# The first sixteen attention items with the exponential taken out of PSUM and the value product turned; a second weight piece in every second preamble round

## The chip, the cores and the metric

The kernel runs on one core of one Trainium2 chip. The metric is the device time of one execution in microseconds (us), median of three runs. The engines are TensorE (PE in the profile; its weight loads are listed apart as PEld), VectorE (DVE), ScalarE (ACT), GpSimd (POOL) and SyncE (SP), which here only issues DMAs. Each engine works off its own instructions in a fixed order.

## What is computed

A causal attention with a window of 128 keys and a linear distance bias, and behind it two two-layer MLPs with the same 2304 tokens, all in float32:

```python
# attention: q, k, v of shape (4, 8, 576, 64)
scores = scale * np.matmul(q, k.transpose(0, 1, 3, 2))
scores = np.where(mask, scores + bias[None], -1000000000.0)
scores = scores - np.max(scores, axis=-1, keepdims=True)
attn = np.exp(scores)
attn = attn / (np.sum(attn, axis=-1, keepdims=True) + 1e-09)
out = np.matmul(attn, v)          # then heads side by side: 2304 tokens x 512
# first MLP, 512 -> 2048 -> 512
h = x @ w_in
g = np.maximum(h, 0.0) + alpha * np.minimum(h, 0.0)
x = g @ w_out
# second MLP, 512 -> 2048 -> 512
h = x @ w_in
g = h * (1.0 / (1.0 + np.exp(-1.702 * h)))
out = g @ w_out
```

## The kernel before

The attention is cut into 64 **items**, one for a batch, a query range (unit 0: 256 queries, unit 1: 320 queries) and a head. Items 0 to 15 (`n < FP`), the heads of the first two batches, are the **float32 items**: their matmuls run on float32 operands. Later items split each operand into a rounded high and a low part and multiply with both. A pair of items (two neighbouring heads) fills one of four 128-row slices of the input `x` of the first MLP, again as high part `xh` and low part `xl`.

One float32 item goes through these steps before the change. `a_qk` (L342) makes the scores of two chunks of 128 queries, 128 and 256 keys wide, in PSUM. `a_bias` (L362) adds the bias on VectorE, writes `tt` in SBUF and leaves the row minimum of the negated scores in `st`. `a_exp` (L378) takes the exponential on ScalarE with the minimum as bias and gathers the row sums. `a_recip` (L386, L387) and `a_norm` (L398) divide on VectorE. `a_trans` (L411) turns three 128x128 blocks on TensorE into PSUM, `a_pt_hi` (L418) copies them to `pt`, and `a_av` (L432) multiplies: the values, laid into one half of a 128-wide tile `vz` whose other half is zero, are the stationary operand, and the product of two heads accumulates to 128 rows by 256 queries, the layout that the MLP wants. `a_x3` (L479, L107) casts it to `xh` and `xl`.

The MLP weights come in as 64-bit numbers and are decoded on the chip. The first MLP has 32 **pieces**, two for each of its 16 slices `f` of the hidden dimension (one of `w_in`, one of `w_out`). A piece costs two ScalarE passes (`w_scale`, L147 and L150), a shift (L154) and an add (L159) on VectorE, and the split into a high part `wh` (a cast, L102 on ScalarE, for two pieces L103 on VectorE) and a low part `wl` (L107 on VectorE).

The program begins with a **preamble** of ten rounds (L741). A round issues the steps of several items, each at another stage, and one weight piece; rounds 0, 4 and 8 issue a second piece. Then the first MLP runs over nine blocks of 256 tokens, each in 16 steps. Step `(k, f)` issues the hidden matmuls of slice `f` (`m1_h`, L493, tile `h`), the activation (L508, L518), its split (`gh`, L522, and `gl`, L107) and, two slices later, the output matmuls (`m1_o`, L544). In block `k = 0` the rest of the 32 pieces is decoded, and half an attention item goes with each step. A scheduler takes the written program and moves instructions of each engine ahead of one another; only the weight steps keep their written order among themselves. So the order on the engines isn't the order in the text.

## Time and profile before

| | us |
|---|---|
| median of 3 runs | 948.61 |
| the three runs | 948.21, 948.61, 950.05 |
| profiled execution, time | 951.22 |
| profiled execution, span | 949.4 |
| TensorE busy | 926.7 (98% of the span) |
| VectorE busy | 687.6 (72%) |
| ScalarE busy | 526.7 (55%) |

The profile is one execution. Its own time of 951.22 lies 2.61 above the median, and 1.8 us of it lie outside the span. Busy shares are means over very different stages: the second MLP fills the last 400 us and has little for VectorE and ScalarE to do, while in the first 105 us VectorE and ScalarE are nearly full. Stretches in time, and the chain of waits, tell more than the means.

### The profile page before, as it was taken

Reading aid. Unit: us, or ns where it says so; the run is one execution under the profiler, and the core shown is the slowest. Engines: PE = TensorE matmul, PEld = TensorE weight load, DVE = VectorE, ACT = ScalarE, POOL = GpSimd, SP = SyncE. Lnnn points to the kernel's source line nnn. Section 1 sums busy time; section 2 is a strip of 40 time slices with the busy share of each in tenths; the row PEclk is TensorE's granted clock in tenths of the full one; section 3 lists DMA queues with packets and bytes.
Section 4 is the critical chain, followed back from the end, with each engine's and each line's share of the span. In section 5 each row is a group of like instructions: output and inputs, shape, how many; then the busy total and the mean of one; then the engine's idle time right before and its main releaser. Section 6 shows DMA issues by size and latency. Waiting matters only on the chain.

```text
span 949.4 us, 17872 instructions
## 1 busy us (share of the span) xinstructions
PE 926.7 (98%) x6536; PEld 862.2 (91%) x6536; DVE 687.6 (72%) x1743; ACT 526.7 (55%) x1325; POOL 89.7 (9%) x127
## 2 busy tenths in 40 slices
PE   6899999999999999999999999999999999999997
PEld 3698899999999999999988888888898899999997
DVE  6898876778888888888457753685333798878876
ACT  5999866667667676676344443564232553433333
POOL 1100211122222222222000000000000000000000
PEclk9999999999999999999999999999999999999999
DMA  9666511223222222221023344665332333433323
GB/s 242 205 217 209 183 54 55 66 68 91 69 67 91 67 68 91 67 90 44 1 89 110 112 128 169 203 227 199 117 124 99 134 134 117 151 133 132 132 72 112
DMA packets 44041, 112.45 MB, mean 118 GB/s; under 512 B 5041, under 2 KB 15153, under 8 KB 43953
## 3 DMA queue, kind: packets, MB, share of 16 engines
q1 hardware_dynamic: 43952, 111.31, 36.1%
q8 instruction: 51, 0.84, 0.4%
q14 instruction: 38, 0.30, 0.1%
HBM read 82.98 MB, written 28.31 MB: 117 GB/s over the span
## 4 chain that ended last, share of the span: by engine, by line
PE 91%; DVE 2%; issue 1%; ACT 0%; DVEq 0%; ACTq 0%
PE h L493 21%; PE h L591 21%; PE p L658 18%; PE o L544 17%; PE p L544 5%; PE x L444 3%; PE pt L411 3%; PE s L351 1%; PE s L352 1%; PE s L342 1%; DVE wl L107 0%; DVE wd L159 0%; ACT oh L102 0%; PE x L432 0%; DVE wd L154 0%
## 5 line engine op out<-in xcount | busy, mean ns | idle before, releaser
L493 PE MATMUL h<-xh,wh 128*128 128x256 f32 (+1 forms) x512 | 151.9, 298 | 1.4 <-ACT xh L479 1.4
L493 PE MATMUL h<-xh,wl 128*128 128x256 f32 (+1 forms) x512 | 152.3, 298 | 0.0
L493 PE MATMUL h<-xl,wh 128*128 128x256 f32 (+1 forms) x512 | 151.4, 296 | 0.0
L658 PE MATMUL p<-wh,oh 128*128 128x256 f32 x504 | 136.3, 284 | 1.0 <-ACT oh L102 0.6
L658 PE MATMUL p<-wl,oh 128*128 128x256 f32 x504 | 136.2, 283 | 0.0
L544 PE MATMUL o<-gh,wl 128*128 128x256 f32 x448 | 127.5, 286 | 0.0
L544 PE MATMUL o<-gh,wh 128*128 128x256 f32 x448 | 125.9, 286 | 0.7 <-ACT gh L522 0.7
L544 PE MATMUL o<-gl,wh 128*128 128x256 f32 x448 | 125.5, 281 | 1.1 <-DVE gl L107 1.1
L658 PE MATMUL p<-wh,ol 128*128 128x256 f32 x504 | 119.2, 283 | 0.4 <-DVE ol L107 0.4
L591 PE MATMUL h<-x2h,wh 128*128 128x512 f32 (+1 forms) x320 | 117.9, 368 | 0.0
L591 PE MATMUL h<-x2l,wh 128*128 128x512 f32 (+1 forms) x320 | 117.8, 368 | 0.0
L591 PE MATMUL h<-x2h,wl 128*128 128x512 f32 (+1 forms) x320 | 117.7, 368 | 0.0
L605 DVE TENSOR_TENSOR g<-h,sg 128x512 f32<-128x512 f32 (+1 forms) x80 | 51.0, 638 | 90.7 <-ACT sg L601 90.5
L601 ACT ACTIVATE sg<-h 128x512 f32<-128x512 f32 (+1 forms) x80 | 44.4, 555 | 108.5 <-PE h L591 108.3
L493 PEld LDWEIGHTS h<-xh,wh 128*128 128x128 f32 x512 | 96.3, 189 | 5.2 <-ACT xh L479 1.9
L493 PEld LDWEIGHTS h<-xh,wl 128*128 128x128 f32 x512 | 96.6, 189 | 3.9 <-DVE wl L107 0.6
L493 PEld LDWEIGHTS h<-xl,wh 128*128 128x128 f32 x512 | 97.0, 189 | 3.0 <-issue 0.3
L658 PEld LDWEIGHTS p<-wh,oh 128*128 128x128 f32 x504 | 96.5, 192 | 2.1 <-ACT oh L102 2.0
L658 PEld LDWEIGHTS p<-wl,oh 128*128 128x128 f32 x504 | 96.7, 192 | 0.1
L518 DVE SCALAR_TENSOR_TENSOR g<-n,beta,h 128x256 f32<-128x256 f32 x112 | 53.2, 475 | 54.1 <-ACT n L508 53.8
L508 ACT ACTIVATE n<-h 128x256 f32<-128x256 f32 x112 | 42.8, 383 | 87.8 <-PE h L493 87.3
L658 PEld LDWEIGHTS p<-wh,ol 128*128 128x128 f32 x504 | 86.5, 192 | 0.7 <-DVE ol L107 0.6
(105 smaller groups left out, 2203.0 us busy)
## 6 DMA issues: line engine op xcount, KB each, us to landing
ws<-in_w_in_dram SPq DMA_DIRECT2D x32, 512.0 KB, 3.9
ws<-in_w_out_dram SPq DMA_DIRECT2D x32, 512.0 KB, 3.7
raw<-in_u_dram SPq DMA_DIRECT2D x32, 512.0 KB, 3.5
g2d<-g SPq DMA_DIRECT2D x32, 512.0 KB, 3.1
gr<-g2d SPq DMA_DIRECT2D x32, 512.0 KB, 3.2
raw<-in_u_dram SPq DMA_DIRECT2D x16, 320.0 KB, 2.8
wd<-x2d SPq DMA_DIRECT2D x36, 128.0 KB, 2.9
out_dram<-ob SPq DMA_DIRECT2D x16, 256.0 KB, 3.4
```

The source lines that it names most:

```text
L342: nc.tensor.matmul(o[:, :keys], raw[:, c0 : c0 + rows], raw[:, 256 + kk : 256 + kk + keys], start=True, stop=True)
L351: nc.tensor.matmul(o[:, :n_], q, kh[:, ks : ks + n_], start=True, stop=False)
L411: nc.tensor.transpose(banks[bank][:, dst : dst + P], src, ident)
L444: nc.tensor.matmul(x[:, oc : oc + nq], v, p[:, col : col + nq], start=(i == 0 and k == 0), stop=(i == len(js) - 1 and k == 1), skip_group_ ...
L493: nc.tensor.matmul(ph, w[:, 0, c * P : (c + 1) * P], x[:, c, r : r + n], start=(c == 0 and i == 0), stop=(c == NC - 1 and i == 2),)
L508: nc.scalar.activation(n, ph, AF.Relu, scale=-1.0)
L518: nc.vector.scalar_tensor_tensor(g, n, beta[:, f : f + 1], ph, op0=ALU.mult, op1=ALU.add)
L544: nc.tensor.matmul(o, w[:, 1, c * P : (c + 1) * P], g, start=(f == 0 and (k == KM or c % 2 == 0) and i == 0), stop=(f == NF - 1 and i == 2 ...
L591: nc.tensor.matmul(ph[:, :n], w[:, f % 2, c * P : (c + 1) * P], x[:, c, :n], start=(c == 0 and i == 0), stop=(c == NC - 1 and i == 2),)
L601: nc.scalar.activation(sg[:, :n], ph[:, :n], AF.Sigmoid, scale=1.702)
L605: nc.vector.tensor_tensor(g[:, f % 2, :n], ph[:, :n], sg[:, :n], op=ALU.mult)
L658: nc.tensor.matmul(o[:, m, :], g[:, a, m * P : (m + 1) * P], w, start=(p == 0 and m == 0 and i == 0), stop=(p == NF // 2 - 1 and i == 2), ...
```

## The change

For the float32 items, the order of the steps is turned around. `f_sub` subtracts from the row minimum (one chunk on VectorE, L383, one on ScalarE, L381) in place of the exponential. The three blocks are transposed unnormalised, and `f_exp` (L389) takes the exponential of the transposed scores straight out of PSUM on its way to `pt`, so that it takes the place of the copy. `f_av` (L463) makes the blocks of `pt` the stationary operand and streams the values, 64 columns and one column of ones, so that the row sums come out as column 65. `f_div` (L474 to L476) divides once for a pair of heads, straight out of PSUM into `xq`, and two more transposes (L520) bring the result into the layout of `x`. The recip and norm steps, and the row-sum reads behind the exponential, fall away for these items. An item is one round shorter: what belonged to item `n - 2` now belongs to `n - 1`. And the preamble's second piece comes in rounds 0, 2, 4, 6 and 8.

```diff
@@ f_sub, f_exp
+            if i:
+                nc.scalar.activation(t, t, AF.Identity, bias=s[:rows, i : i + 1], scale=-1.0)
+            else:
+                nc.vector.tensor_scalar(t, t, s[:rows, i : i + 1], -1.0, op0=ALU.subtract, op1=ALU.mult)
...
+            x, c, w = st["t", n][0]
+            nc.scalar.activation(pts[n % 2], x[:, :w], AF.Exp)
@@ f_av, f_div in place of a_av for these items
+        if h % 2 == 0:
+            st["xq", n // 2] = early("o0", n, "xq").rearrange("p c (h t) -> p c h t", h=2)
+        x = st["xq", n // 2]
+        pt, vz = pts[n % 2], vzs[n % 2]
+        for c, j, col in ((0, 0, 0), (1, 0, 128), (1, 1, 256)):
+            nc.tensor.matmul(
+                x[:, c, h % 2, : D + 1], pt[:, col : col + P], vz[:, j, :],
+                start=(c == j == h % 2 == 0), stop=(c == j), skip_group_check=True,
+            )
...
+        nc.vector.tensor_scalar(r, x[:, :, :, D], 1e-9, None, op0=ALU.add)
+        nc.vector.reciprocal(f, r)
+        nc.vector.tensor_tensor(xq, x[:, :, :, :D], f.unsqueeze(3).to_broadcast([P, 2, 2, D]), op=ALU.mult)
-            for j in range(2):
-                nc.tensor.matmul(
-                    x[:, j * P : 256], vz[:, j, :], pt[:, j * 256 : 256 + j * P],
...
@@ a_x3
-            xp = st["x", n]
+            xp = early("o1", n, "x").rearrange("p c t -> p (c t)")
+            for i in range(2):
+                nc.tensor.transpose(xp[:, i * P : (i + 1) * P], xq[:, i, :, :], ident)
@@ the preamble's rounds
-        a_av(n - 2)
+        f_exp(n - 1)
         a_split_v(n)
...
         a_bias(n)
+        f_sub(n)
         w("split")
-        a_exp(n)
-        a_recip(n - 1)
+        f_av(n - 1)
         w("shift")
-        a_norm(n - 1, "dve")
-        a_trans(n - 1)
         w("add")
         w_ahead()
+        f_div(n - 1)
+        a_trans(n, True)
         w("scale")
-        a_x3(n - 2)
-        if n % 4 == 0:
+        if n % 2 == 0:
             w("split")
             w("shift")
-        a_pt_hi(n - 1, 0)
-        a_pt_hi(n - 1, 1)
+        a_x3(n - 1)
```

`early` takes a PSUM bank that the first MLP's output sums use only later (for items 0 to 7) or one of the four attention banks. In block `k = 0` the float32 items 10 to 15 go the same new way.

The scheduler's order moves with it. On VectorE, the first MLP's first block can start once the fourth `xl` is written, the slice of heads 6 and 7. In these rows `wl` with a number is the low half of the weights of one slice `f`, `st` the row statistics, `g` and `gl` the activation and its low half. Before, VectorE at the fourth `xl`, with ten `wl` already written:

```order
L159 ISA wd<-ws,wd 128x1024 x2
L386 TENSOR_SCALAR st_149<-st_149 128x2
L387 RECIPROCAL st_149<-st_149 128x2
L398 TENSOR_SCALAR tt_147<-tt_147,st_149 128x128
L398 TENSOR_SCALAR tt_147<-tt_147,st_149 128x256
L107 TENSOR_TENSOR xl<-x,xh 128x256
L107 TENSOR_TENSOR wl_498<-wd,wh_497 128x512
```

Now, VectorE at the fourth `xl`, with nine `wl` already written:

```order
L474 TENSOR_SCALAR st_149<-xq 128x4
L159 ISA wd<-ws,wd 128x1024
L475 RECIPROCAL st_149<-st_149 128x4
L476 TENSOR_TENSOR xq<-xq,st_149 128x256
L107 TENSOR_TENSOR wl_432<-wd,wh_431 128x512
L154 TENSOR_SCALAR wd<-wd 128x512
L362 ISA tt_146,st_148<-s,relht 128x128
L362 ISA st_148 128x1
L362 ISA tt_146,st_148<-s,relht 128x256
L362 ISA st_148 128x1
L107 TENSOR_TENSOR xl<-x,xh 128x256
```

The normalising pair L398 is gone there, and the division of a pair (L474 to L476) stands in its place. The other place is VectorE at the last pieces of the first MLP's weights, those of slice 15, whose first `wl` (of `w_in`) the hidden matmuls of step `(0, 15)` need. Before, `wl_1123` being slice 14 and `wl_1229` slice 15:

```order
L107 TENSOR_TENSOR wl_1123<-wd,wh_1122 128x512
L362 ISA tt_147,st_149<-s,relt 128x128
L362 ISA st_149 128x1
L362 ISA tt_147,st_149<-s,relt 128x256
L362 ISA st_149 128x1
L107 TENSOR_TENSOR wl_1123<-wd,wh_1122 128x512
L107 TENSOR_TENSOR wl_1229<-wd,wh_1228 128x512
L107 TENSOR_TENSOR gl<-g,gh 128x256
L107 TENSOR_TENSOR ptl<-pt,pth 128x384
```

Now, with `wl_1080` slice 14 and `wl_1140` slice 15; `xp` and `ptl`, `q` are steps of the split items behind the float32 ones:

```order
L107 TENSOR_TENSOR wl_1080<-wd,wh_1079 128x512
L154 TENSOR_SCALAR wd<-wd 128x512
L565 SCALAR_TENSOR_TENSOR g<-n,beta,h 128x256
L362 ISA tt_147,st_149<-s,relt 128x128
L362 ISA st_149 128x1
L362 ISA tt_147,st_149<-s,relt 128x256
L362 ISA st_149 128x1
L510 TENSOR_TENSOR xp<-x,tb 64x256
L159 ISA wd<-ws,wd 128x1024
L107 TENSOR_TENSOR wl_1140<-wd,wh_1139 128x512
L318 SCALAR_TENSOR_TENSOR q<-raw_144,q 64x256
L107 TENSOR_TENSOR ptl<-pt,pth 128x384
```

The `wl` of slice 15 moved behind steps of four more split items: by then 22 items have passed the bias step, before it was 18. On TensorE the same has happened: ahead of the first matmul that reads the low half of slice 15 there now stand 12 hidden and 12 output matmuls more of the MLP, 12 more transposes, and the score and value matmuls of four split items. Before, TensorE at that matmul (`wl_1229`):

```order
L544 MATMUL o_696<-gh,wh_1059 128x256
L544 MATMUL o_697<-gh,wh_1059 128x256
L444 MATMUL x<-pth,vp_1318 128x256
L493 MATMUL h<-xh,wl_1229 128x256
L493 MATMUL h<-xh,wh_1228 128x256
```

Now (`wl_1140`), with the hidden matmuls of the next block (`wl_232`) ahead of it:

```order
L540 MATMUL h<-xh,wl_232 128x256
L489 MATMUL x<-pth,vp_1321 128x256
L591 MATMUL o_717<-gh,wh_1079 128x256
L591 MATMUL o_718<-gh,wh_1079 128x256
L540 MATMUL h<-xh,wl_1140 128x256
L540 MATMUL h<-xh,wh_1139 128x256
```

The row moved from 6008 matmuls before the end to 5940. Further down, the last 5696 TensorE rows stand in the same order in both kernels.

## Rows read from the trace of the kernel before

**Rows 1.** Stretches: us; busy us of PE, PEld, DVE, ACT, POOL; clock, DMA.

```profile
10.00:47.00 37.00, 30.70 (x115) 21.70 (x116) 31.19 (x107) 31.10 (x82) 4.54 (x10) 1.00 0.81 225
47.00:90.00 43.00, 42.99 (x320) 38.85 (x321) 38.84 (x112) 38.60 (x96) 2.94 (x7) 1.00 0.66 211
90.00:105.10 15.10, 12.54 (x88) 10.79 (x86) 14.94 (x45) 14.99 (x40) 2.28 (x5) 1.00 0.74 233
105.10:946.00 840.90, 837.19 (x6009) 788.99 (x6008) 599.97 (x1471) 438.53 (x1102) 77.56 (x92) 1.00 0.32 106
```

**Rows 2.** Waits of PE from 105.2 to the end: us, times, longest.

```profile
PE p L658 <- ACT oh L102: 0.6, 1, 0.6
PE p L658 <- DVE ol L107: 0.4, 1, 0.4
```

**Rows 3.** Timeline: start, us, engine, line, op; the fourth `xl`, last pieces, matmul behind.

```profile
46.85 0.42 DVE L107 TENSOR_TENSOR xl<-x,xh 128x256 fp32r<-128x256 f32 x1
...
103.78 1.28 DVE L107 TENSOR_TENSOR wl<-wd,wh 128x512 fp32r<-128x512 f32 x2
...
105.12 0.39 PE L493 MATMUL h<-xh,wl 128*128 128x256 f32 x1
```

**Rows 4.** Chain that ended last, 85 to 112 us: start, us to the next step.

```profile
85.49 0.65 PE x L432 x4
...
90.04 0.34 DVE tt L362
90.39 0.60 DVE wl L107
90.99 0.34 DVE wd L154
91.33 0.39 DVE g L518
91.72 0.60 DVE wd L159
92.32 0.08 DVE st L386
...
93.54 0.46 DVE tt L398 x2
...
95.93 0.20 DVE tt L362
...
97.12 0.36 DVE q L317
...
99.54 0.34 DVE gl L107
...
100.61 0.41 issue
...
101.52 0.14 issue
...
108.07 1.45 PE h L493 x12
...
111.40 0.09 PE s L351
...
111.61 0.22 PE pt L411 x2
```

**Rows 5.** ACT groups, 9 to 105.1: shape, count, busy us, mean ns, idle before.

```profile
L378 ACT ACTIVATE tt<-tt,st 128x256 f32<-128x256 f32 x17 | 8.5, 503 | 0.0
L378 ACT ACTIVATE tt<-tt,st 128x128 f32<-128x128 f32 x17 | 6.8, 403 | 0.0
L378 ACT ACTIVATION_READ_ACCUMULATOR tt<-tt,st 128x1 f32 x33 | 6.4, 194 | 0.0
```

**Rows 6.** One PE shape, first from 3 to 32, then from 33 to 100 us.

```profile
L342 PE MATMUL s<-raw 64*128 64x256 f32 x8 | 4.2, 631 | 0.0
...
L342 PE MATMUL s<-raw 64*128 64x256 f32 x16 | 5.0, 390 | 0.0
```

More of the change, by code (lines that the diff above doesn't have):

```diff
@@ L373, in a_exp, with f_sub, f_exp @@
     @stage
+    def f_sub(n, b, u, h, U):
+        if n >= FP:
+            return
+        tt, s = tts[n % 2], sts[n % 2]
+        for i, (c0, rows, kk, keys) in enumerate(U["chunks"]):
+            t = tt[:rows, i * 256 : i * 256 + keys]
+            if i:
+                nc.scalar.activation(t, t, AF.Identity, bias=s[:rows, i : i + 1], scale=-1.0)
+            else:
+                nc.vector.tensor_scalar(t, t, s[:rows, i : i + 1], -1.0, op0=ALU.subtract, op1=ALU.mult)
+    @stage
+    def f_exp(n, b, u, h, U):
+        if n < FP:
+            x, c, w = st["t", n][0]
+            nc.scalar.activation(pts[n % 2], x[:, :w], AF.Exp)
+    @stage
     def a_exp(n, b, u, h, U):
         tt, s = tts[n % 2], sts[n % 2]
+        if n < FP:
+            return
         for i, (c0, rows, kk, keys) in enumerate(U["chunks"]):
@@ L391, in a_norm @@
         tt, s = tts[n % 2], sts[n % 2]
-        for i, (c0, rows, kk, keys) in enumerate(U["chunks"]):
+        for i, (c0, rows, kk, keys) in enumerate(U["chunks"] if n >= FP else ()):
             t = tt[:rows, i * 256 : i * 256 + keys]
@@ L415, in a_pt_hi @@
     def a_pt_hi(n, b, u, h, U, i):
-        if i <= u:
+        if i <= u and n >= FP:
             x, c, w = st["t", n][i]
-            nc.scalar.copy(pts[n % 2] if n < FP else ar["pth"][:, c : c + w], x[:, :w])
+            nc.scalar.copy(ar["pth"][:, c : c + w], x[:, :w])
     @stage
@@ L424, in a_pt_lo, with early, f_av, f_div @@
             sub("dve", ar["ptl"][:, c : c + w], x[:, :w], ar["pth"][:, c : c + w])
+    def early(tag, n, name):
+        pool, tag = (pso, tag) if n < H else (ps_a, "a")
+        return pool.tile([P, 2, T1], F32, tag=tag, name=name)
+    @stage
+    def f_av(n, b, u, h, U):
+        if n >= FP:
+            return
+        if h % 2 == 0:
[7 more added lines that the diff above has]
+            )
+    @stage
+    def f_div(n, b, u, h, U):
+        if n >= FP or h % 2 == 0:
+            return
+        s, x = sts[n % 2], st["xq", n // 2]
+        r, f = (s[:, i : i + 4].rearrange("p (c h) -> p c h", c=2) for i in (8, 12))
+        nc.vector.tensor_scalar(r, x[:, :, :, D], 1e-9, None, op0=ALU.add)
+        nc.vector.reciprocal(f, r)
+        nc.vector.tensor_tensor(xq, x[:, :, :, :D], f.unsqueeze(3).to_broadcast([P, 2, 2, D]), op=ALU.mult)
     @stage
@@ L707, in tile_window_attention__then__two_mlps @@
     for t in vzs:
-        nc.gpsimd.memset(t, 0.0)
+        nc.gpsimd.memset(t, 1.0)
     for t in sts:
@@ L778, in tile_window_attention__then__two_mlps @@
     a_split(n)
-    for i in range(2):
-        a_pt_lo(n - 2, i)
-    a_recip(n - 1)
-    a_norm(n - 1, "dve")
-    a_av(n - 2)
-    a_x1(n - 2)
-    a_x2(n - 2)
-    a_x3(n - 2)
+    f_exp(n - 1)
     at0.close()
```

28 lines of the change are left out of this document (18 added, 10 removed).

## The prediction

> **What bounds the kernel now.** I read the busy times by stretch first [rows 1]. From 105.1 us on TensorE is busy without a break: 6009 matmuls, 837.2 of 840.9 us, and in all that time it waits 1.0 us for other engines [rows 2]. Nothing that VectorE or ScalarE saves there shortens anything. Ahead of that point TensorE has gaps: 6.3 us of 37 between 10 and 47, none between 47 and 90, 2.6 of 15.1 between 90 and 105.1 [rows 1]. In this last stretch VectorE and ScalarE are full (14.94 and 14.99 of 15.1), and the chain of waits runs over VectorE, with weight steps, bias, split, and two short pauses in it [rows 4]. The last gap ends at one instruction. VectorE writes two `wl` from 103.78 to 105.06, the second is the low half of `w_in` for slice 15, and at 105.12 TensorE starts the hidden matmul that reads it [rows 3]. From there the order of all TensorE work is a full queue. So the time is the moment at which this `wl` is there, plus the TensorE work that stands behind the matmul that reads it. I predict these two numbers and nothing else.
>
> **What of the change costs nothing.** GpSimd's memset and value copies (POOL is busy 4.54 of 37 us early on [rows 1]) and the DMA issues on SP, which carry the same transfers in nearly the same order, are covered; uncovered, a late value copy would hold only the value product of one item. Past the point where the orders agree again the kernels are the same, TensorE is full there, and VectorE's lighter queue is worth zero.
>
> **VectorE's queue up to the fourth `xl`.** With it the first block of the MLP can start; it begins at 46.85 before [rows 3]. I count what the order puts ahead of it, and price each kind by its distance to the next start in the chain [rows 4]: `wl` 0.60, add 0.60, shift 0.34, a 256-wide operation on two tensors 0.34, bias 0.34 and 0.20 for its two chunks, the 256-wide half of the normalising pair 0.46 - 0.20 = 0.26, a row-statistics step 0.08, of which I make 0.10 for the dependent ones. Away: 10 normalising halves (2.6), 12 statistics steps net (1.2), 3 adds, 2 shifts and 1 `wl` (3.1, only put off). New: 4 divisions (1.4; the trace has none, and `gl`, of the same shape out of PSUM or SBUF, is the nearest row; 0.3 to 0.5 each) and one more bias (0.5). Sum: -5.0 us, so with the same pauses the block starts at 41.8. The 128-wide subtraction costs what the 128-wide half of the normalising pair cost.
>
> **VectorE's queue up to the deciding `wl`.** The same count there: away 12 normalising halves (3.1) and 8 statistics steps (0.8). New: 8 divisions (2.7), one add, shift and `xl` (1.3), one `g` and `gl` (0.7), and the steps of four more split items: 4 biases (2.2), 4 normalising 128-wide halves (0.8), 4 `q` (0.36 each, 1.4), 4 `xp` (1.4) and 4 `ptl`, 384 wide (0.47 each as an estimate from the 256-wide 0.34; 1.9). Sum: +8.5 us. The count says what the diff doesn't: the float32 items get cheaper, but the scheduler uses the room to draw four later items in front of the last weights.
>
> **TensorE's queue behind that matmul** gets shorter for the same reason: 68 rows fewer. 24 MLP matmuls at 1.45/12 = 0.12 (2.9), 12 transposes at 0.11 (1.3), 16 score and 16 value matmuls, half of them 192 wide at 0.09 and half 256 wide at 0.12 (3.4) [rows 4]. Sum: -7.6 us. So with unchanged pauses on VectorE the two sums nearly cancel: +8.5 - 7.6 = +0.9.
>
> **The pauses.** VectorE idles 4.3 us between 47 and 105.1 (43.0 - 38.84 and 15.1 - 14.94) [rows 1], because TensorE, full from 47 to 90, is the bound there for a while. In this stretch the two queues are nearly equal now: TensorE 55.5, VectorE 53.8 of 58.1 us. After the change VectorE has 5.0 + 8.5 = 13.5 more in it, 67.3. TensorE gets the 7.6 from above and 8 transposes (0.9), loses 7 float32 value products at 0.65 (4.6) [rows 4] and gets 18 of the 128x65 products. The trace has no such shape. Each is two passes, as the four of the old item's two products show; a transpose is one pass of 128 columns at 0.11, so two passes of 65 columns lie between 0.11, if only the columns count, and 0.22, if the weight load of each pass does: 2.0 to 4.0 us. TensorE: +5.9 to +7.9, about 62.4. VectorE is then clearly the longer one, and waits less for TensorE. I let half of the 4.3 us go, -2.1; bounds 0 and 4.3. ScalarE doesn't step in: 12 128-wide exponentials with two sum reads each go away, which by 0.40 and 0.19 less the 0.1 that successive starts overlap is 6.0, 4 256-wide passes come (1.6), and 22 others of at most about 0.40 [rows 5], 8.8: at most +4.4, half of VectorE's +8.5.
>
> Before 47 VectorE idles 5.8 of 37 us [rows 1]. TensorE runs there at the lower of its two levels (1.2 GHz by its durations): the same score matmul takes 631 ns up to 32 us and 390 later [rows 6], though the clock column reads 1.00. The new order has one transposing step more per pair and smaller value products, so TensorE's part is about even, but new links (division, transposes, cast) come in. I take 0 for it, between -1.2 and +1.5.
>
> **The sum.** +8.5 - 7.6 - 2.1 = -1.2 us on the profiled execution's 951.2, 950.0. The profiled execution lies 2.6 above the median of 948.6; the same step from the median is 947.4.
>
> **Rivals.** First, VectorE never waits for TensorE in the stretch. For it: TensorE's queue is then 5 us the shorter one. Against: shorter only in sum; the first slices after the block's start find their weights decoded, and there TensorE is the late one. All 4.3 us go: +0.9 - 4.3 = -3.4, 945.2.
>
> Second, slower: the links. A split item's exponential, reciprocal, normalising, transposes and `ptl` go back and forth between the engines, and one such chain stands in front of the deciding `wl` today, with pauses of 0.41 and 0.14 on VectorE [rows 4]. Four more come in front, 4 x 0.55 = 2.2, and each of eight divisions waits for a value product and hands on to two transposes and a cast with little between. If these links add 2.2 to the 4.3 instead of taking 2.1 off: +0.9 + 2.2 = +3.1, 951.7. It decides once VectorE's pauses in the stretch pass 5.3 us (0.9 + 1.0 = 1.9, or 0.2%). Against: most links have a weight step in between in the order.
>
> Third, TensorE stays at its lower level for longer. The level rose at about 32 us after a stretch in which TensorE was busy nearly without a pause. In the new order the preamble's TensorE work holds more transposes and value products of half the columns. If the rise waits until the first block at 41.8, some 9.5 us more run at the level at which the 5.8 us of pauses arose; at 5.8 in about 22 us that is 2.5 us, and up to 5 if TensorE alone sets the pace. I take 3.7: 951.1. Against: the MLP's first matmuls stand ahead in the preamble as before, and TensorE is hardly less busy. The Trainium skill (TensorE: Matmul & The Clock Gate, Part 4: PE-mode transpose) says that transposes don't count as busy in the same way for the clock gate; by that rule this third case is what happens. Rows 6 show only that the level did rise in a preamble with three transposes an item, which speaks against the rule's full force here.
>
> **How the numbers follow.** The forecast's case 0.53, around 947.4 with 945.5 to 949.5 for its own bounds; the first rival 0.24, the second 0.16, the third 0.07. A measurement of this kernel can tell about 0.2% (1.9 us: 946.7 and 950.5) from no change. The forecast's case lies with 0.17 below 946.7 and 0.36 within; the first rival with 0.20 below and 0.04 within; the second with 0.12 above and 0.04 within; the third with 0.05 above and 0.02 within. Rounded, with a hundredth for what I don't see: faster 0.37, same 0.45, slower 0.18. The range for 8 in 10 leaves out the tails of the first and second rival: 944.0 to 951.3.
>
> **What would show it.** In the changed profile: the fourth `xl` near 41.8 (40.5 to 43.5); the deciding `wl` ending near 111.5 (105.06 + 8.5 - 2.1), TensorE full from there on, with 5940 matmuls; VectorE's pauses between the block's start and that `wl` near 2 us; 128x65 products starting 0.06 to 0.11 apart per pass; the score matmul falling to 390 ns near 32 us. The sum is wrong if TensorE waits for something else after the deciding `wl`, since then both counts are taken at the wrong place; if ScalarE's casts `wh` come later than VectorE can use them; or if the fourth `xl` isn't early.

## The result and the profile after

The changed kernel takes 962.16 us (959.92 to 962.80, four runs), the kernel before 949.33 in the same comparison: a ratio of 1.0122, 95% interval 1.0099 to 1.0145. The forecast was 947.4, with 944.0 to 951.3. The change makes the kernel about 12 us slower, and the forecast missed both the sign and the range. The profiled execution of the changed kernel has a span of 960.8 us against 949.4, 11.4 more; all sums below are made on that difference.

The stretches answer to [rows 1]; the columns are the same. The last one begins where TensorE's last early gap ends.

```profile
10.00:47.00 37.00, 35.50 (x150) 27.42 (x149) 25.69 (x89) 24.61 (x50) 4.28 (x11) 1.00 0.73 211
47.00:90.00 43.00, 40.84 (x313) 37.30 (x313) 38.55 (x111) 36.42 (x83) 4.06 (x7) 1.00 0.62 197
90.00:123.80 33.80, 26.71 (x176) 24.03 (x174) 32.59 (x93) 30.62 (x84) 9.10 (x13) 0.90 0.62 195
123.80:957.00 833.20, 829.84 (x5940) 781.37 (x5940) 586.33 (x1422) 426.74 (x1059) 72.00 (x83) 1.00 0.32 105
```

The picture has turned over. Between 10 and 47 us TensorE was the engine with gaps (6.3 us), VectorE and ScalarE were the busy ones (31.2 and 31.1 of 37). Now TensorE is busy 35.5 of 37, and VectorE and ScalarE stand still for 11.3 and 12.4 us. From 47 on it is the other way round: TensorE has gaps of 2.2 us up to 90 and 7.1 up to 123.8, where it had 2.6 in all, and VectorE is nearly full. Note the clock of 0.90 in the third stretch; in the kernel before it reads 1.00 throughout.

The timeline answers to [rows 3]: the fourth `xl`, the last `wl` that TensorE waits for, and the matmul that reads it.

```profile
47.31 0.41 DVE L107 TENSOR_TENSOR xl<-x,xh 128x256 fp32r<-128x256 f32 x1
...
123.08 0.68 DVE L107 TENSOR_TENSOR wl<-wd,wh 128x512 fp32r<-128x512 f32 x1
...
123.81 0.38 PE L540 MATMUL h<-xh,wl 128*128 128x256 f32 x1 [0.31 <-DVE wl L107]
```

That matmul is the one the prediction named, with 5940 matmuls from it to the end, and from there on TensorE is full. It starts 18.7 us later than before (105.12). The fourth `xl` comes at 47.31 in place of 46.85, so the first MLP block starts no earlier.

What TensorE waits for between 10 and 200 us (total, times, longest):

```profile
PE h L540 <- ACT wh L102: 5.7, 5, 2.1
PE h L540 <- DVE wl L107: 1.2, 3, 0.5
...
PE pt L435 <- DVE tt L420: 0.8, 1, 0.8
```

Before, the 3.5 us on `pt` were the largest of these waits and none was on a weight's cast. Now it is the weights. VectorE's waits up to 47.3 us, first after, then before:

```profile
DVE tt L362 <- PE s L342: 10.1, 6, 5.4
DVE wl L107 <- ACT wh L102: 4.7, 4, 2.4
DVE wd L154 <- ACT wd L147: 2.3, 1, 2.3
```

```profile
DVE tt L362 <- PE s L342: 6.6, 2, 5.4
DVE tt L362 <- PE pt L411: 3.3, 3, 1.7
```

The 5.4 us are the start of the program in both. What is new is that VectorE waits four times more for scores that TensorE hasn't reached, and for `wh`.

The level of TensorE's clock can be read from equal instructions. The first four lines are around its first rise, the others around two later falls (start, duration):

```profile
37.08 1.65 PE L342 MATMUL s<-raw 64*128 64x128 f32 x4
...
39.57 0.41 PE L540 MATMUL h<-xl,wh 128*128 128x256 f32 x1
...
43.13 0.28 PE L540 MATMUL h<-xh,wl 128*128 128x256 f32 x1
...
45.31 0.92 PE L342 MATMUL s<-raw 64*128 64x128 f32 x4
...
94.17 0.38 PE L540 MATMUL h<-xh,wh 128*128 128x256 f32 x1 [1.70 <-ACT wh L102]
...
95.78 0.28 PE L540 MATMUL h<-xl,wh 128*128 128x256 f32 x1
...
96.24 0.41 PE L540 MATMUL h<-xl,wh 128*128 128x256 f32 x1
...
109.20 0.39 PE L540 MATMUL h<-xh,wh 128*128 128x256 f32 x1 [2.13 <-ACT wh L102]
...
111.04 0.41 PE L540 MATMUL h<-xl,wh 128*128 128x256 f32 x1
...
113.47 0.28 PE L591 MATMUL o<-gh,wh 128*128 128x256 f32 x1
```

A hidden matmul of 0.41 us (0.21 apart) is one at the lower level (1.2 GHz), one of 0.28 (0.12 apart) one at the higher (2.4 GHz). The first rise lies near 41.4 us, where [rows 6] have it near 32. At 96.0 us, after a gap of 1.70 us for `wh`, the granted clock falls to 0.50 for 3.4 us; after the gap of 2.13 it falls again, from 109.7 to 113.1. The profiled execution of the kernel before has no such fall.

### The profile page after: what moved, and what is told of

The parts are those of the page before. It is cut to its first block, busy times and chain, and to the rows that moved or that the text cites. A ratio compares the mean times of both kernels' runs of the same rounds, so it can differ in the third digit from the quotient of the medians.

```text
span 960.8 us, 17871 instructions
## 1 busy us (share of the span) xinstructions
PE 936.9 (98%) x6584; PEld 872.5 (91%) x6584; DVE 685.7 (71%) x1719; ACT 521.3 (54%) x1277; POOL 91.3 (10%) x127
## 4 chain that ended last, share of the span: by engine, by line
PE 91%; DVE 3%; ACT 3%; issue 1%; DMA 1%; SPq 0%; DVEq 0%; ACTq 0%
PE h L540 20%; PE h L638 20%; PE p L705 18%; PE o L591 16%; PE p L591 5%; PE x L489 3%; PE pt L435 3%; PE s L342 2%; PE s L351 1%; PE s L352 1%; PE xq L463 1%; DVE wl L107 1%; DMA rawf<-in_u_dram 1%; ACT ws L150 1%; ACT wh L102 1%
## 5 line engine op out<-in xcount | busy, mean ns | idle before, releaser
L540 PEld LDWEIGHTS h<-xh,wh 128*128 128x128 f32 x512 | 97.0, 190 | 11.7 <-ACT wh L102 6.8
```

The source lines that it names most:

```text
L540: nc.tensor.matmul(ph, w[:, 0, c * P : (c + 1) * P], x[:, c, r : r + n], start=(c == 0 and i == 0), stop=(c == NC - 1 and i == 2),)
```

## The experiments

All kernels in one table. The ratio is to the kernel before in the same comparison, with its 95% interval. "Rise" is the first change of TensorE to its higher level, where equal instructions get shorter as above; "falls" are later stretches at a granted clock of 0.50. "Pieces" are the `wl` written ahead of the fourth `xl`. The last two columns are TensorE's busy time in the whole span and its pauses from 10 to 130 us. All columns behind the ratio are of the one profiled execution.

| kernel | us | ratio | fourth `xl` | pieces | rise, falls (us) | busy | pauses |
|---|---|---|---|---|---|---|---|
| before | 949.3 | 1 | 46.9 | 10 | 32 | 926.7 | 8.9 |
| after | 962.2 | 1.0122 (1.0099 to 1.0145) | 47.3 | 9 | 41; 96-99, 110-113 | 936.9 | 10.8 |
| turned_only | 958.2 | 1.0090 (1.0068 to 1.0112) | 43.1 | 8 | 32; 80-83, 97-100 | 931.1 | 12.1 |
| rate_only | 949.8 | 1.0004 (0.9993 to 1.0015) | 49.1 | 12 | 34; 41-48 | 927.9 | 6.2 |
| wide | 962.7 | 1.0131 (1.0112 to 1.0150) | 41.2 | 7 | 26; 88-91, 104-111, 118-122 | 933.4 | 15.0 |
| xmm | 956.6 | 1.0069 (1.0048 to 1.0089) | 46.9 | 10 | 42 | 935.2 | 6.7 |
| warm | 966.1 | 1.0162 (1.0133 to 1.0192) | 49.7 | 8 | 5, again 53; 12-53, 87-90 | 941.7 | 11.2 |
| warm_before | 955.2 | 1.0057 (1.0035 to 1.0078) | 51.3 | 10 | 5, again 49; 11-49 | 936.0 | 6.8 |
| hold | 959.2 | 1.0081 (1.0053 to 1.0108) | 47.3 | 9 | 41; 89-92, 96-99 | 936.0 | 9.9 |
| hold_before | 949.0 | 0.9989 (0.9977 to 1.0001) | 44.3 | 10 | 24; 38-44, 92-96 | 926.1 | 7.1 |
| lean | 962.3 | 1.0125 (1.0109 to 1.0142) | 47.2 | 9 | 42; 83-86, 103-106 | 935.9 | 10.1 |
| lean_wide | 965.1 | 1.0153 (1.0132 to 1.0174) | 39.9 | 7 | 26; 74-80, 91-94, 121-125 | 935.0 | 16.3 |
| norm_pool | 949.1 | 0.9992 (0.9980 to 1.0003) | 42.9 | 10 | 23; 43-47 | 923.2 | 9.0 |
| norm_pool2 | 953.0 | 1.0029 (1.0015 to 1.0042) | 45.5 | 10 | 33; 47-57 | 929.5 | 7.6 |
| loaded | 961.6 | 1.0117 (1.0091 to 1.0142) | 64.6 | 16 | 75 | 942.1 | 7.9 |
| pinx | 960.0 | 1.0098 (1.0076 to 1.0121) | 54.6 | 12 | 42; 52-59 | 934.9 | 9.6 |
| loaded_wide | 961.3 | 1.0109 (1.0094 to 1.0124) | 61.6 | 16 | 25; 42-63, 66-73 | 931.8 | 14.3 |
| loaded_lean | 963.0 | 1.0132 (1.0115 to 1.0149) | 57.2 | 16 | 29; 42-59, 63-66 | 932.0 | 8.4 |
| light | 944.5 | 0.9934 (0.9906 to 0.9962) | 41.3 | 11 | 29 | 923.8 | 0.6 |
| light_before | 939.1 | 0.9889 (0.9872 to 0.9906) | 39.1 | 10 | 23 | 920.0 | 3.6 |

The scheduler orders every one of these programs anew, so an edit also moves rows that it doesn't name. That limits what a single run can tell.

### The two halves of the change

turned_only is after with `if n % 4 == 0`, rate_only is before with `if n % 2 == 0`, each in both places that issue the second piece.

```diff
-        if n % 2 == 0:
+        if n % 4 == 0:
             w("split")
             w("shift")
...
-        if n % 2 == 0:
+        if n % 4 == 0:
             w("add")
             w_ahead()
```

> The kernel after, with the second weight piece again in every fourth preamble round (rounds 0, 4, 8): the turned product alone. Theory A (clock): most of the 11.4 us between the two profiled spans (960.8 and 949.4) is TensorE time at its lower level, because the score matmul stays at 631 ns until 38.7 us instead of 32, and because the level falls again for 3.3 us at 96.0 and at 110.1, behind gaps. The new products stand in the preamble whatever the piece rate is, so the 631 ns should last until 38 to 42 us here too, and the time is 955 to 962. Theory B (the pieces): the two extra pieces give ScalarE more to do before 60 us and make its casts late after 75 us, 5.7 us of TensorE waits on them. Then the time falls to about the kernel before's, 947 to 951, and the waits on the weight cast go under 1.5 us, even if the clock rises late.

> The kernel before, with a second weight piece in every second preamble round instead of every fourth, and the old value product: the piece rate alone. Theory A (clock, caused by the new value product): the score matmul falls from 631 to about 377 ns near 32 us as before, there is no stretch at the lower level after it, and the time is within 2 us of the kernel before's, 947 to 951. Theory B (the pieces): TensorE waits for weight casts of ScalarE in the stretch from 75 to 125 us, 3 us or more in sum, and the time is 953 or more.

The turned product alone costs 8 us, the piece rate alone nothing, and together 12. So the turned product is the cause; whether the earlier pieces make it worse in its company isn't clear, since the intervals of turned_only and after overlap. What the run calls the product is all of the change but the piece rate: the value product, the two transposes behind it, the item that is one round shorter and the other PSUM banks. No run takes these apart.

Theory A has the time of turned_only right, but not its ground. Scores on TensorE in turned_only, and what TensorE waits for from 47 to 130 us:

```profile
26.85 1.65 PE L342 MATMUL s<-rawf 64*128 64x128 f32 x4
...
34.76 0.92 PE L342 MATMUL s<-raw 64*128 64x128 f32 x4
```

```profile
PE h L540 <- ACT wh L102: 5.5, 3, 2.3
PE h L540 <- DVE tt L420: 2.3, 1, 2.3
```

The level rises at 32 us, as early as in the kernel before and not at 38 to 42, the fourth `xl` comes 3.8 us sooner than there, and still 8 us are lost, behind the block's start. Theory B fails too: the waits on the weight casts stay at 5.5 us without the extra pieces. rate_only is a miss for theory A in one point: its level fell for 7 us from 41 on, behind a gap of 1.97 us, and the time stayed.

### TensorE's level

wide makes the value passes 128 columns wide; xmm turns the quotient with plain matmuls; warm and warm_before add ten matmuls of zeros to TensorE's first idle stretches.

```diff
-    vzs = [apf.tile([P, 2, D + 1], F32, name=f"vz{i}") for i in range(2)]
+    vzs = [apf.tile([P, 2, P], F32, name=f"vz{i}") for i in range(2)]
...
-                x[:, c, h % 2, : D + 1], pt[:, col : col + P], vz[:, j, :],
+                x[:, c, h % 2, :], pt[:, col : col + P], vz[:, j, :],
```

> The kernel after, with the value product's moving side 128 columns wide instead of 65 (the further 63 hold ones and are not read). A pass of the 65-wide product took 0.195 us at the lower level and 0.105 at the higher one, a 128-wide transpose 0.21 and 0.11: if a pass costs what its weight load costs, the wider one costs at most 0.015 us more each, under 1 us in all. Theory A1 (the clock doesn't rise because passes of 65 columns leave TensorE half idle between weight loads): the score matmul gets to 377 ns at 32 to 35 us instead of past 38.7, and the time falls by 3 to 5 us to 957 to 959. Theory A2 (the clock doesn't rise because there are more transposes and fewer plain matmuls, or for another reason): the rise stays at 39 to 42 us and the time within 2 us of 962. The order of rows moves a little in this kernel as well, which alone could give 2 us either way.

The timeline of wide around its rise, and two of its stretches:

```profile
22.00 2.76 PE L463 MATMUL xq<-vz,pt 128*128 128x128 f32 x12
...
25.54 1.13 PE L342 MATMUL s<-rawf 64*128 64x128 f32 x4
...
28.68 0.83 PE L463 MATMUL xq<-vz,pt 128*128 128x128 f32 x6
```

```profile
47.00:90.00 43.00, 38.71 (x284) 35.07 (x283) 39.10 (x111) 35.38 (x83) 5.92 (x10) 0.97 0.60 198
90.00:117.00 27.00, 18.62 (x120) 17.06 (x118) 23.48 (x65) 23.32 (x61) 4.80 (x7) 0.86 0.58 184
```

The four scores from 25.54 on take 1.13 us, on the way from 1.65 to 0.92: the level rises 15 us sooner. The fourth `xl` comes 6.1 us sooner too, 3.5 of it because VectorE pauses less ahead of it (15.6 us in place of 19.1), so TensorE at its lower level did hold the preamble; the rest goes with two pieces fewer ahead of it. But the time is the same. What TensorE wins it loses behind the block's start, with gaps of 4.3 and 8.4 us in these two stretches, and three falls of the level behind gaps. Theory A1 had the direction of the rise right and the time wrong.

```diff
-                nc.tensor.transpose(xp[:, i * P : (i + 1) * P], xq[:, i, :, :], ident)
+                nc.tensor.matmul(
+                    xp[:, i * P : (i + 1) * P], xq[:, i, :, :].rearrange("p h d -> p (h d)"), ident,
+                    start=True, stop=True, skip_group_check=True,
+                )
```

> The kernel after, with the two turns of the quotient per pair as ordinary float32 matmuls against the identity, in place of transposes: the same result, two passes in place of one, 0.42 us more per pair at the lower level. Theory A2 (more transposes hold the clock down): the score matmul gets to 377 ns clearly earlier than 39 us, at 32 to 37, and the time falls by 2 to 4 us less 1 us for the passes, 957 to 961. Theory A1 (the 65-wide passes): the rise stays at 39 to 42 us and the time is 961 to 964. Theory B (the pieces): no change beyond 2 us.

The rise is at 42 us as in after, so the two added transposes aren't what keeps the level down. Yet the time is 5.5 us lower, below every range given, with no later fall and 4 us less of pauses. The edit moves the order throughout; which part of that brings the 5.5 wasn't found.

```diff
+    z = first.tile([P, 512], BF16, name="z")
+    nc.vector.memset(z, 0.0)
+    def warm(m):
+        o = ps_a.tile([P, 512], F32, tag="a", name="warm")
+        for _ in range(m):
+            nc.tensor.matmul(o, z[:, :P], z, start=True, stop=True, skip_group_check=True)
...
+    warm(6)
     a_qk(0)
+    warm(4)
```

> The kernel after with ten extra matmuls of a zero tile (128x512, bfloat16) in TensorE's first idle stretches, six ahead of the first scores and four between the first and the second; their product isn't read. They should lift TensorE's level long before 41.5 us, without narrowing anything else; the order behind is a little different: by the count VectorE's work up to the deciding wl is 3.0 us less, TensorE's work behind 1.3 us more. Theory C (TensorE at its lower level fills the preamble, and VectorE's pauses there, 6.0 us more up to the fourth xl than before, come from that): the level is up before 20 us, the fourth xl comes near 41 in place of 47.3, VectorE's pauses fall by 4 to 8 us and the time by 6 to 9, 953 to 956. Pure queue theory (pauses given back later anyway, as in the kernel with 128-wide passes, whose level rose at 26 us and whose time was 962.7): -1.7, 959 to 962. Pure clock theory (all the time at the lower level is lost time): 950 or less.

> The kernel before with the same ten extra matmuls. By the count the queues move by +0.4 us. Theory C: in the kernel before VectorE is the longer queue in the preamble, its pauses that wait for TensorE between 10 and 47 us are 3.3 us, so at most that goes: 946 to 949. Pure clock theory: the kernel before spends about 23 us busy at the lower level, which cost it some 10 us: 941 or less. If the level doesn't rise early, 949 to 951 and the run says nothing.

Both went against every expectation, above all ranges: the level was up from about 5 us, fell at 11.7 and 11.4 us behind gaps of 1.64 (warm) and 2.54 us (warm_before), and then stayed low until 52.6 and 49.0 us. That makes warm_before the best test of the level alone, since by the count its queues are those of the kernel before within 0.4 us. Its stretches:

```profile
10.00:20.00 10.00, 8.64 (x26) 5.71 (x27) 8.43 (x29) 8.57 (x23) 0.72 (x2) 0.57 1.05 289
20.00:47.00 27.00, 24.83 (x76) 17.05 (x76) 18.33 (x66) 18.20 (x48) 2.97 (x7) 0.50 0.62 182
47.00:52.00 5.00, 4.56 (x21) 3.61 (x21) 4.33 (x13) 4.78 (x12) 0.81 (x2) 0.80 0.30 77
```

From 20 to 47 us the clock is 0.50, TensorE is nearly full, and VectorE and ScalarE idle 8.7 and 8.8 of 27 us, as in the kernel after. The fourth `xl` is 4.5 us later than in the kernel before, and the span 5.2 us longer (954.6 against 949.4). So a later lasting rise, by 16 us, costs the kernel before some 5 us, and does it through the pauses of the other engines. Short falls tell less: of 58 executions of the kernel before, 39 have a mean granted clock of 0.995 or 0.996, and 19 one of 0.998 or 0.999, which is what the profiled execution without a fall has; the median times are 950.8 and 950.0 us.

### VectorE's queue and the split items

hold pins the `q` step of the split items behind the weight steps; hold_before does so in the kernel before.

```diff
-        nc.scalar.mul(qst[:, :nq], raw[:, :nq], sc)
+        pin(nc.scalar.mul(qst[:, :nq], raw[:, :nq], sc))
...
-        nc.vector.scalar_tensor_tensor(
+        pin(nc.vector.scalar_tensor_tensor(
...
```

> The kernel after, with the q step of the split items (ScalarE's L316 and VectorE's L317) pinned behind the weight steps that stand ahead of it in the program, so that in the first MLP block no split item is drawn ahead of the last weights. The preamble's order is unchanged. Queue theory: the time moves with VectorE's work ahead of the deciding wl plus the TensorE work behind the matmul that reads it, plus VectorE's pauses. By the order and the durations of the profile of after, VectorE's work up to that wl is 104.9 us in place of 116.7 (36 bias chunks ahead in place of 44) and TensorE has 4.5 us more behind it: -7.3, the time 953 to 957. Clock theory (the late rise of TensorE's level at 41.5 us is what costs): the rise is where it was, and only the two later falls can go (3.2 us): 959 to 963.

> The kernel before with the same pins. Queue theory: VectorE's work up to the deciding wl 104.2 in place of 105.8 us, TensorE 0.3 less behind it: -1.9, the time 946.5 to 949 where the kernel before has 949 to 950. If the pins cost something of their own (ScalarE or VectorE standing still at a pinned step), the time is 951 or more.

VectorE's waits in hold from 75 to 117 us:

```profile
DVE wl L107 <- ACT wh L102: 3.1, 4, 1.4
DVE xl L107 <- ACT xh L526: 0.9, 1, 0.9
DVE wd L154 <- ACT wd L147: 0.7, 2, 0.4
```

Up to TensorE's last early gap VectorE's work is 88.3 us in place of 99.1 and TensorE has 5.5 us more behind it, which would give -5.3; but VectorE's pauses grow by 3.5, to 28.2. It now waits for the two ScalarE steps of a piece, which wait for VectorE's. The gain is 3.0 us by the medians and 1.8 by the profiled spans, and the intervals of hold and after overlap, where the queue theory said 7.3; the time is just inside the clock theory's range. So the queue theory falls. That the piece's own chain is the next bound is what the waits suggest; no run shows it alone. In the kernel before the same pins move the time by no more than the measurement tells (949.0 against 950.3).

lean and lean_wide take VectorE work away; norm_pool and norm_pool2 do so in the kernel before.

```diff
-                nc.vector.tensor_scalar(t, t, s[:rows, i : i + 1], -1.0, op0=ALU.subtract, op1=ALU.mult)
+                nc.gpsimd.tensor_scalar(t, t, s[:rows, i : i + 1], -1.0, op0=ALU.subtract, op1=ALU.mult)
...
-        nc.vector.tensor_scalar(r, x[:, :, :, D], 1e-9, None, op0=ALU.add)
-        nc.vector.reciprocal(f, r)
+        nc.vector.reciprocal(f, x[:, :, :, D])
```

> The kernel after with less VectorE work for the same result: the 128-wide subtraction of the float32 items on GpSimd (16 steps of 0.29 us), and the division's step that adds 1e-9 left out (8 of 0.16; the row sum is at least one, so the float32 sum doesn't change). By the order and the durations, VectorE's work up to the deciding wl is 107.4 us in place of 116.7, TensorE has 1.3 more behind it: -8.0. Of it 3.6 lie ahead of the fourth xl, where TensorE at its lower level is the longer queue, and 4.4 behind it. Theory C: the first part turns into pauses, the second counts: 956 to 959. Pure queue theory: 953 to 955. If the time is set by something else (ScalarE's weight casts, TensorE's level), 960 to 963.

> The same two savings in the kernel with 128-wide value passes, whose level rose at 26 us and which took 962.7. By the count -6.7, of it 3.9 ahead of the fourth xl, which is at 41.2 us there. Theory C, with TensorE at its higher level from 26 us on: VectorE is again the longer queue for a part of the preamble, 955 to 959. Pure queue theory: 956. If ScalarE is next, 960 to 963.

> The kernel before with the 128-wide half of the float32 items' normalising step on GpSimd in place of VectorE, 16 steps of 0.29 us. By the count VectorE's work up to the deciding wl is 101.9 in place of 105.8 us and TensorE has 1.2 less behind it: -5.1, of it 2.9 ahead of the fourth xl. Queue theory: 944 to 946. If the first part turns into pauses: 946 to 948. If the gain goes to ScalarE (14.99 busy of 15.1 us in the last stretch): 948 to 951.

> The kernel before with both halves of the float32 items' normalising step on GpSimd, 16 of 0.29 and 16 of 0.35 us. By the count -12.8 us, of it 6.4 ahead of the fourth xl. TensorE's gaps from 10 to 105 us are 8.9 us in the kernel before, so no more than that can come from gaps; ScalarE is busy 53.6 of the 58.1 us from 47 to 105.1 and becomes the bound. Queue theory with ScalarE next: 942 to 946. GpSimd's longer steps stand in each item's chain (normalise, transpose, copy): if that chain sets the preamble, 948 or more.

Stretches of lean, and GpSimd's new steps in it:

```profile
10.00:47.00 37.00, 36.57 (x154) 28.76 (x154) 24.39 (x77) 24.38 (x50) 11.28 (x22) 1.00 0.73 197
47.00:115.40 68.40, 58.80 (x425) 53.37 (x423) 60.59 (x165) 58.21 (x141) 13.00 (x21) 0.95 0.63 202
```

```profile
L383 POOL TENSOR_SCALAR tt<-tt,st 128x128 f32<-128x128 f32 x16 | 11.5, 722 | 33.8 <-DVE st L362 33.8
```

Nothing is won in any of the four. In lean, norm_pool and norm_pool2 the last case of the expectation came, in which something else is the bound; lean_wide lies above all of its cases. Moved to GpSimd, the 128-wide step takes 0.72 us where VectorE takes 0.29, and it stands in every item's chain. So these runs don't separate less work on VectorE from a longer chain. VectorE does less and pauses more: up to TensorE's last early gap, its work in lean is 87.1 us (12.0 less), its pauses are 28.3 (3.5 more), and TensorE has 7.0 us more behind. So less work on VectorE doesn't by itself shorten the kernel after or the one before. For the preamble the first of lean's stretches shows why: TensorE is busy 36.57 of 37 us.

### The weight pieces

loaded has a second piece in all ten rounds, and the casts of the input pinned behind the weights; pinx has the pins alone; loaded_wide and loaded_lean add the edits of wide and of lean.

```diff
-        if n % 2 == 0:
+        if True:
             w("split")
...
-            nc.scalar.copy(xh[:, c, r : r + w], xp[:, done : done + w])
-            sub("dve", xl[:, c, r : r + w], xp[:, done : done + w], xh[:, c, r : r + w])
+            pin(nc.scalar.copy(xh[:, c, r : r + w], xp[:, done : done + w]))
+            pin(sub("dve", xl[:, c, r : r + w], xp[:, done : done + w], xh[:, c, r : r + w]))
```

> The kernel after with a second weight piece in all ten preamble rounds, and with the input's cast (xh, xl) pinned behind the weight steps that stand ahead of it in the program: 16 pieces are decoded ahead of the fourth xl in place of 9. Nothing of the float32 items is changed. Theory D (the room that the cheaper items leave in the preamble isn't used: VectorE pauses 19.1 and ScalarE 19.9 us up to the fourth xl, and behind it each piece takes 3.4 us while TensorE starves and its level falls): the fourth xl comes later, 50 to 56 us, but TensorE has under 4 us of gaps behind it and no fall of its level; VectorE's count is 8.9 us shorter; the time 946 to 953. Level theory (the long start at the lower level costs by itself): the preamble gets no shorter, the rise no earlier, and the time stays at 959 to 964.

> The kernel after with the same pin of the input's cast, and the second piece in rounds 0, 2, 4, 6 and 8 as it is: 12 pieces ahead of the fourth xl in place of 9. The order alone. Theory D: a part of the way from after to the front-loaded kernel, by the count -4.8 us, 954 to 958, with 5 us or less of gaps in TensorE behind the fourth xl (9.1 in after). Level theory: 960 to 964.

> The front-loaded kernel with value passes of 128 columns in place of 65. Theory D with the level on top: with the pieces in the preamble, an earlier rise (26 us in the kernel with wide passes) now counts, 1 to 4 us below the front-loaded kernel. If the level doesn't matter: within 1 us of it. If VectorE fills the preamble now, TensorE pauses in it and the rise may not come early: then within 1 us as well.

> The front-loaded kernel with the two savings on VectorE (16 subtractions on GpSimd, 8 additions left out). By the count VectorE's work up to the deciding wl falls by 9 us more. Theory D: with VectorE the longer queue in the preamble now, a part of that counts, 2 to 6 us below the front-loaded kernel; with ScalarE next, 0 to 2. In the kernel after the same savings gave nothing.

In loaded TensorE has 1.9 us of gaps between the fourth `xl` and its last gap, as theory D has it. But the fourth `xl` comes at 64.6 us, not at 50 to 56, and the level rises at 75 only; its busy time grows to 942.1. In this execution the starving is gone, and the lower level has taken its place. It took 965.5 us; the other three took 960.0 to 961.7 at a mean granted clock of 0.980 to 0.985 in place of 0.999, so their level took another course. In loaded_wide the level rises at 25 us, falls at 42 at the start of a wait of 7.9 us for the input's cast, and the time is within 1 us of loaded's, as the expectation's last two cases have it. pinx is 2 us better than after where 4.8 were expected, and its interval overlaps that of after. loaded_lean misses: its median is 1.3 us above loaded's, where 0 to 6 below were expected. Its row in the table is of an execution of 955.4 us, with the other four at 962.9 to 964.5; why they lie so far apart wasn't found. So theory D by itself falls too. That pieces, level and items' chains bind each other is the reading that is left, and it isn't shown.

The last pair leaves ScalarE's second pass and VectorE's add out of every piece, in both kernels. Their weights lack the low words, so the pair tells of the cause and offers no faster kernel.

```diff
-        pin(nc.scalar.mul(lo, lo.bitcast(U32), 2.0**-29))
...
-        pin(nc.vector.tensor_tensor(wtm[i], wtm[i], lo, op=ALU.add))
```

> The kernel after without the low words of the weights: ScalarE's second pass (0.67 us a piece) and VectorE's add (0.70) are left out, for all pieces. So a piece takes a third less of both engines and its chain is two steps shorter. TensorE's work is unchanged. Piece theory (behind the preamble TensorE waits for the chain of the weight pieces, and the level falls in those waits): gaps behind 47 us under 3 us in place of 9.3, no fall of the level, and the time 6 to 13 us below the kernel after, 949 to 956. Level theory (the late rise costs): 10 us of difference to the next kernel stay.

> The kernel before with the same steps left out. Piece theory: it has 2.6 us of gaps behind 47 us to lose and some in the preamble, 944 to 948; the difference to the kernel above is then 2 to 6 us, of which 1.5 are TensorE's own extra work and the rest the later rise. Level theory: 940 to 944, 10 us or more below the kernel above.

The stretches of light:

```profile
10.00:47.00 37.00, 36.38 (x190) 28.52 (x189) 29.50 (x106) 27.51 (x59) 5.31 (x13) 1.00 1.00 284
47.00:90.00 43.00, 43.00 (x350) 41.27 (x349) 35.13 (x98) 33.27 (x77) 3.54 (x6) 1.00 0.82 252
```

and of light_before:

```profile
10.00:47.00 37.00, 33.42 (x163) 24.75 (x164) 31.29 (x119) 30.57 (x88) 4.71 (x12) 1.00 0.96 290
47.00:90.00 43.00, 43.00 (x333) 40.12 (x332) 38.49 (x111) 36.73 (x97) 5.14 (x10) 1.00 0.75 250
```

With the weights' decoding lightened, TensorE is full from 47 us on in both, no level falls, and light takes 17.6 us less than after, light_before 9.7 less than before (948.77 in that comparison). What is left between them is 5.5 us by the medians and 0.4 by the profiled spans (938.3 and 937.9). The two figures differ because light's five executions lie in two groups, 939.5 to 940.4 and 944.5 to 945.4, and the profiled one is of the first. In both readings more than half of the 12 us depends on the decoding of the weights: the turned product is nearly free, or costs half, where the weights are in time. The pair takes work off two engines and steps out of the piece's chain at once, and in light the level rises at 29 us in place of 41, so it doesn't tell which of these it is. The medians' difference lies in the 2 to 6 us that the piece theory gave; both times are lower than it said.

## Why the prediction was wrong

**The frame.** The prediction wrote the time as VectorE's queue up to one `wl`, its pauses, and TensorE's work behind the matmul that reads it. These terms add up to the span of any kernel, so that the sum closes proves nothing; their sizes do. Measured on the two profiles, with the stretches cut at 105.1 and 123.8 us:

| term | forecast | measured | from |
|---|---|---|---|
| VectorE's work up to that `wl` | +8.5 | +11.4 | 87.6 to 99.1 |
| TensorE from that matmul to the end | -7.6 | -7.3 | 844.3 to 837.0 |
| VectorE's pauses up to the fourth `xl` | 0 | +5.9 | 13.2 to 19.1 |
| VectorE's pauses from there on | -2.1 | +1.4 | 4.3 to 5.7 |
| sum | -1.2 | +11.4 | 949.4 to 960.8 |

**TensorE behind the matmul: right**, to the matmul (5940), and with it the count that the scheduler draws four more split items in front.

**VectorE's work: sign and cause right, 2.9 us too small.** Taken by kind up to that `wl`, each step at its length or its distance to the next start, whichever is less, most of the prices hold: the biases came to +2.1 us (2.2 forecast), `ptl` to +1.9 (1.9), the normalising halves of 256 to -3.3 (-3.1), the divisions less the statistics to +1.8 (1.9). Too small were `g` and `gl` (+1.9 for 0.7), `q` (+2.1 for 1.4), the 128-wide halves (+1.4 for 0.8) and, by less, `xp` and the weight steps. Groups of VectorE in after, 9 to 124 us:

```profile
L107 DVE TENSOR_TENSOR gl<-g,gh 128x256 fp32r<-128x256 f32 x14 | 6.9, 495 | 0.0
L476 DVE TENSOR_TENSOR xq<-xq,st 128x256 f32<-128x256 f32 x8 | 3.4, 421 | 0.2
L475 DVE RECIPROCAL st<-st 128x4 f32<-128x4 f32 x8 | 1.4, 172 | 0.1
L474 DVE TENSOR_SCALAR st<-xq 128x4 f32<-128x4 f32 x8 | 1.2, 152 | 1.1 <-PE xq L463 1.1
```

The same 14 `gl` took 418 ns each in the kernel before; why they take longer wasn't found. A quotient is 0.42 us long and its next start 0.34 behind, the price that was taken, where the next step follows at once. In front of a wait a step counts with its whole length, and VectorE waits 61 times up to that `wl` where it waited 49 times before. The work ahead of the fourth `xl` was right: -5.5 us against -5.0.

**The pauses: the step that failed.** It is the one sentence "I take 0 for it, between -1.2 and +1.5", with its ground, "TensorE's part is about even"; VectorE's pauses up to the fourth `xl` grew by 5.9 us. The saved 5 us were to bring the fourth `xl` to 41.8; it came at 47.31, and the saving became a pause. VectorE's queue no longer set the preamble's end. TensorE did, full at its lower level until 41.4 us, and its part wasn't even: ahead of the fourth `xl` it is busy 39.8 us where it was 33.8, with 38 transposes in place of 28 and the scores of eleven items in place of ten. The numbers for a warning stood in the prediction: an engine with 6.3 us of gaps in 37, at half its rate, is not far from being the bound itself once another one gets 5 us shorter.

The late rise isn't the whole of it. In turned_only the level rises at 32 us and the fourth `xl` comes at 43.1, in wide at 26 and 41.2. Yet VectorE's pauses up to TensorE's last early gap grow by 5.7 and 6.6 us over the kernel before, 3.1 and 4.2 of them behind the fourth `xl`, where the forecast had -2.1. So the two pause terms, -2.1 together in the forecast, came out at +7.3 in after and some 6 with an early rise as well: a saving ahead of the block turned into waits behind it.

**TensorE's new passes: at the dear end of the bounds.** Value products of after at the lower and at the higher level, in the chain of waits:

```profile
13.10 1.18 PE xq L463 x6
...
61.75 0.61 PE xq L463 x6
```

A pass of 65 columns takes 0.20 us and 0.10. One of 128 columns takes 0.21 and 0.11 in wide (2.55 us for twelve, 0.67 for six). Half the columns save next to nothing, so the turned product with its transposes is no lighter for TensorE than the old one: 6 rows and one transpose of 0.11 against 0.65 for 4 rows [rows 4], +0.07 an item, 1.1 in all.

**TensorE's account** of the same 11.4 us: busy +10.2 (926.7 to 936.9), pauses +1.2. Of the busy time 1.1 is that extra work; the two falls, 6.8 us at half rate, make about 2.9, as an estimate from 0.21 against 0.12 a matmul; ahead of its first rise TensorE is busy 34.5 us where it was 23.3, and these 11.2 make about 4.8 by the same estimate; 1.4 stay unassigned. The pauses only moved, from the preamble (4.8 less from 10 to 47) to the stretch behind it (6.7 more).

**The rivals.** The first, no pauses left, was the opposite of what came. The second, links, was right in kind: the pauses in the stretch grew by 1.4 us where it said 2.2. The third named something that happened, the rise at the first block (41.4 against the 41.8 of the text), but priced it at 3.7 us and gave it 0.07. It left out that a full TensorE makes the saving of VectorE worthless. And the rise can't be the main price: turned_only lost 8 us with a rise at 32. The rule that it cited (the Trainium skill, TensorE: Matmul & The Clock Gate, Part 4: PE-mode transpose) isn't what these runs show as the reason: with the two new transposes as plain matmuls the rise stayed at 42 us, with all transposes in place it came at 32 in turned_only, and with wider value passes at 26. No run replaced the three older transposes of an item.

**What is shown and what stays open.** Shown: the turned product with what comes along with it is the cause and not the piece rate; a rise as early as before doesn't undo the loss; a later rise costs the kernel before some 5 us; an earlier rise, less VectorE work, or more pieces ahead each give nothing or little alone in the kernel after; with the weights' decoding lightened more than half of the loss is gone. Open: which part of the turned product it is, which handoff of a weight piece between ScalarE and VectorE paces the stretch from 47 to 124 us, why xmm's order is 5.5 us better, and why the executions of light and loaded_lean lie 5 to 8 us apart. None of the runs beats the kernel before with the full computation by more than the measurement tells.

## What to carry to other kernels

When an edit makes the busiest engine's queue shorter, work out by how much the next one is longer than what remains, at the rate that the trace shows for that stretch, before the saving is booked; where three engines are nearly full side by side, as here, a saving on one mostly becomes its pause. Counting the changed order gave TensorE's term within 0.3 us and VectorE's within a third, but pauses don't follow from a count, and they deserve the wide part of the range. The distance to the next start prices a step where the next follows at once; in front of a wait the step counts with its whole length.

## What the runs showed of the hardware

- A float32 pass of 65 moving columns takes nearly as long as one of 128: 0.105 against 0.111 us at the higher level.
- TensorE stayed at its lower level although it was busy without a break: in warm, 5.00 of 5 us busy in each stretch from 15 to 50 us at a clock of 0.50, and from 15 to 40 us in after. In wide the level rose at 26 us, in loaded at 75.
- The level fell behind gaps of 1.70 and 2.13 us in after and of 1.97 in rate_only, and in hold behind two of 0.35 and 0.55 close together. It didn't fall behind one of 1.77 in xmm, of 2.45 in warm, or two of 2.33 and 2.34 in turned_only.
- Ahead of the first rise the clock column reads 1.00 although equal matmuls take nearly twice as long; behind a fall it reads 0.50. The durations are the safer sign.
- A 128x128 step on one tensor with one scalar for each row took 0.72 us on GpSimd in lean (0.86 in norm_pool2) and 0.29 on VectorE in after.
